# Products of k and v in unbroken rows, and wide and narrow matmuls in alternation, in a linear-attention and token-mixing block

## The chip, the cores and the metric

The kernel runs on one core of a Trainium2 chip. The core has five engines, each with its own queue in a fixed order: TensorE (PE, whose weight loads are shown as PEld), VectorE (DVE), ScalarE (ACT), GpSimd (POOL) and SyncE (SP), which issues most DMAs. They wait for each other on semaphores. The metric is the device time of one execution in microseconds (us), lower is better.

## The reference

```
def _A_ref(x, wqkv, w_phi, wo):                       # x: (1, 2048, 512), 32 heads of 16
    q, k, v = ...(x @ wqkv)...
    pq = jnp.einsum("bhsd,hdf->bhsf", q, w_phi)
    pk = jnp.einsum("bhsd,hdf->bhsf", k, w_phi)
    phi_q = jnp.concatenate([_softmax(pq, axis=-1), _softmax(-pq, axis=-1)], axis=-1)
    phi_k = jnp.concatenate([_softmax(pk, axis=-1), _softmax(-pk, axis=-1)], axis=-1)
    kv = jnp.einsum("bhsf,bhsd->bhfd", phi_k, v)
    z  = jnp.einsum("bhsf->bhf", phi_k)
    num = jnp.einsum("bhqf,bhfd->bhqd", phi_q, kv)
    den = jnp.einsum("bhqf,bhf->bhq", phi_q, z)[..., None] + 1e-6
    return (num / den)... @ wo
def _B_ref(x, w1, b1, w2, b2):                        # w1: (2048, 1792), w2: (1792, 2048)
    h = _layernorm(x, axis=-1)
    u = _gelu(jnp.einsum("bsd,sf->bdf", h, w1) + b1)
    y = jnp.einsum("bdf,fs->bds", u, w2) + b2
    return y transposed to (B, S, D)
h = x + _A_ref(_layernorm(x, axis=-1), A_wqkv, A_w_phi, A_wo)
h2 = h + _B_ref(_layernorm(h, axis=-1), B_w1, B_b1, B_w2, B_b2)
```

All values are fp32. The first half is a linear attention with a softmax feature map, the second an MLP over the token axis.

## The kernel before

The 2048 tokens are 16 tiles of 128 rows. An fp32 product is done as three products of a split operand: each operand is cut into a high part in the type fp32r and a low part (the rest), and high x high, high x low and low x high are added up in PSUM (`mm3`, L69 to L71: one wide matmul, 128x512, for each). ACT makes high parts and DVE or POOL low parts.

**Attention, about 43 to 140 us.** For each tile PE does projections of 12 wide matmuls: q (`pu`), k (`pk_ps`, already multiplied by the feature map's weights) and v (`pv`). DVE takes the maximum and the minimum of each head (L168, L169) and subtracts (L162, L166), ACT takes the exponential (L188), DVE sums it (L210), POOL normalises pk (L212) and adds it up in `zacc` (L216). ACT writes v as `vs` (L203), and the statistics of the layernorm (`sqj`, L128 and L129) and the splits of x (`xs`, L64) are on ACT too. The products of k and v, `kv(t)`, are 16 small matmuls per tile, of 32 weight columns and 64 moving columns (`kvp`, L224). They are issued in four blocks of four tiles each by `v_kv`. In this stage a scheduler orders each engine's queue: it works from the program's order, priorities and costs of its own, and may put one piece of work between others. At the end of the stage DVE adds the last tile to zacc (L499) and makes its low part (L502), PE sums it over the partitions (L510, L511), ACT writes it as zB (L512), POOL multiplies it with the q features (L461), and DVE goes on from there (L470 to L474).

**First MLP product, up to about 378 us.** It is not touched by the change, but the last stretch of it, 349 to 378 us, is ordered by the scheduler too.

**Second MLP product, from about 378 us on.** The two-by-two block product is done with seven products instead of eight (Strassen's way), so each step issues seven products with sums of blocks as operands. There are eight row blocks (`sp`) with seven steps (`p`) each. One step has six full products (`PROD`, `half` None) and one narrow one (`narrow`). A full product is a wide matmul with the high weights (`whi`, 128x512, the high and the low part of u side by side) and a narrow one with the low weights (`wlo`, 128x256), both by `wide` (L1132). `narrow` (L1136) issues three narrow matmuls. So a step is six wide and nine narrow matmuls. The weights of w2 come in 28 groups of two steps: a DMA, sums on DVE (L875 to L877), the high part by ACT (L1017, three buffers), the low part by DVE (L1027, two buffers). Three places issue the steps: at p = 0 `products` for one step, which for a single step already is wide, narrow, wide, narrow; in the middle `steps`, for one group or half of one; and at the end of a row block `products` for the last two steps (three in the last row block) together. Then ACT (L1193, L1195) and DVE (L1199 to L1204) combine the seven results and the output goes out by DMA. From the first line after `flat` on, PE, DVE and ACT keep the order in which the program is written.

Of the kernel before, what the change touches and what calls it, by code (L numbers as in the profile page):

```python
# [32 lines left out]
TURN = (6, 7, 8)  # L33
DEN_EPS = 1e-6
LAG = 5
WARM = 9
EPS = 1e-5

# [2 lines left out]
def block_kernel(ctx: ExitStack, tc: tile.TileContext, x, xT, wT, phic, wo, w1, b1, w2, b2,  # L41
# [68 lines left out]
    X, XH, EQ, PK, VS, SQ, PS, W = {}, {}, {}, {}, {}, {}, {}, {}  # L110
# [94 lines left out]
    def v_proj(t):  # L205
        v_out(t, proj(t, wvh, wvl, ps_v, "pv"))
# [11 lines left out]
    def kv(t):  # L218

        for n in range(4):  # L220
            for c in range(4):
                g = n // 2 * 4 + c
                j = 2 * g + n % 2
                nc.tensor.matmul(kvp[32 * c:32 * c + 32, n, :], VS[t][:, 32 * j:32 * j + 32],  # L224
                                 PK[t][:, g, n % 2 * 64:n % 2 * 64 + 64], start=(t == 0 and n == 0),
                                 stop=(t == NT - 1), skip_group_check=True)

    def q_sum(t):
# [5 lines left out]
    with tc.tile_pool(name="prep", bufs=1) as prep:  # L234
# [67 lines left out]
        warm = ps_k.tile([P, P], F32, name="pk_ps", tag="pk_ps")  # L302
        for _ in range(WARM):
            nc.tensor.matmul(warm, ones, ones, start=True, stop=True)
# [99 lines left out]
    def v_kv():  # L404

        nonlocal v
        v_proj(v)
        if v % 4 == 0:
            for t in range(v - 4, v):
                kv(t)  # L410
        v += 1

    v = 2
    load_h(4)
    stats_x(4)
    for t in range(3, NT - 1):
        if t + 2 < NT:
            raw = load_x(t + 2)
            load_h(t + 2)
        if t > 3:  # L420
            k_logits(t)
        if t > 3 and t not in V_NOT:
            v_kv()
        if t > 0:
            k_norm(t - 1)
        if t + 2 < NT:
            split_x(t + 2, raw)
            stats_x(t + 2)
        if t in Q_AT:
            q_mm()  # L430
            run(q_logits(0))
            q_exp(0)
            run(q_sums(1))
# [45 lines left out]
    def lead(it, mm):  # L479
# [6 lines left out]
        q_exp(0)  # L486

    v_kv()
    nc.gpsimd.tensor_add(zacc, zacc, PK[NT - 2])
    q_mm()  # L490
    k_norm(NT - 1, False)
    for j in range(KD):
        wo_hi(j)
    v_kv()
    run(q_logits(0))
    zh, zl = (kk.tile([P, NG, P], F32R, name=name, tag="pk", bufs=len(V_NOT) + 5) for name in ("zh", "zl"))
# [32 lines left out]
    for t in range(NT - 4, NT):  # L529
        kv(t)  # L530
# [157 lines left out]
    def fill_load(p):  # L688
        if FL[p] < NT:
            WI[p, FL[p]] = stream(w1v, FL[p], 2, p * 256, 256)  # L690
            FL[p] += 2

    def fill(p, pool=None):

        t = FN[p]
        FN[p] = t + 1
        if FL[p] <= t:
            fill_load(p)
        if any(part is WI[p, t - t % 2][1] for part, _, _ in LATER):
            flush()  # L700
        if t == 0:
            PU[p] = [pool.tile([P, D], F32, name="pu", tag="pu") for _ in range(2)]
        a, b = WI[p, t - t % 2]
        for c in range(2):
            mm3(PU[p][c], a[:, t % 2, c * P:(c + 1) * P], b[:, t % 2, c * P:(c + 1) * P],
                HN[t][:, 0], HN[t][:, 1], t == 0, t == NT - 1)

    def fills(it):
        if FN[1] < it - LAG:
            fill(1, ps_q)  # L710
        if FN[0] <= it - LAG:
            fill(0, ps_f)
# [12 lines left out]
    for it in range(NT + 4):  # L725
# [65 lines left out]
        for p in range(2):  # L791
            if it >= LAG - 3 + p and FL[p] <= FN[p] + 2 * (FN[p] > 0):
                fill_load(p)
# [258 lines left out]
    todo, late = [], []  # L1052
    NEAR_AT, LATE_AT = (1, 4), (2, 3, 4, 6, 8, 10)
    for n, (p, i) in enumerate(RUN):
# [12 lines left out]
        todo = todo[2:]  # L1067
# [51 lines left out]
    def products(sp, ps, order):  # L1119
        for a, b, bk, half in order:  # L1120
            if half is None:
                for low in range(2):
                    for p in ps:
                        wide(sp, p, a, b, bk, low)
            else:
                for p in ps:
                    narrow(sp, p, a, b, bk, half)

    def wide(sp, p, a, b, bk, low):
        w, u = AW[sp, p][low][:, a], UB[p, b]  # L1130
        o, u = (bank[bk][:, 0], u[:, 0]) if low else (bank[bk], u)
        nc.tensor.matmul(o, w, u, start=p == 0 and not low, stop=p == NP - 1, skip_group_check=True)  # L1132

    def narrow(sp, p, a, b, bk, half):
        for i, (x, y) in enumerate(((0, 0), (0, 1), (1, 0))):
            nc.tensor.matmul(bank[bk][:, half], AW[sp, p][x][:, a], UB[p, b][:, y], start=p == 0 and half == 0 and i == 0,  # L1136
                             stop=p == NP - 1 and i == 2, skip_group_check=True)

    def steps(sp, ps, order):
        for p in ps:  # L1140
            for a, b, bk, half in order:
                if half is None:
                    wide(sp, p, a, b, bk, 0)
        for p in ps:
            for a, b, bk, half in order:
                if half is None:
                    wide(sp, p, a, b, bk, 1)
            for a, b, bk, half in order:
                if half is not None:
                    narrow(sp, p, a, b, bk, half)  # L1150
# [6 lines left out]
    for n, (sp, p) in enumerate(STEPS):  # L1157
        t = 2 * sp
# [12 lines left out]
        order = ENDS if last else PROD  # L1171
        run_on = 3 if last else 2
        if p == 0:
            products(sp, [p], order[:-1] if n == 0 else order)
            continue
        if n == 1:
            steps(sp, [p], order[:-1])
            products(sp, [0, p], order[-1:])
            continue
        if p < NP - run_on:  # L1180
            if n % GRP == 0 or p == 1:
                steps(sp, range(p, min(p + GRP - n % GRP, NP - run_on)), order)
            continue
        if p < NP - 1:
            continue
        products(sp, range(NP - run_on, NP), order)
        e = uo.tile([P, 2, HD], F32, name="e")
        u2 = uo.tile([P, HD], F32, name="u2", bufs=1)
        u3 = uo.tile([P, HD], F32, name="u3")
        if not last:  # L1190
            ot = uo.tile([P, 2, 2, HD], F32, name="ot", bufs=1)
            low = uo.tile([P, 3, HD], F32, name="low")
# [100 lines left out]
```

## Time and profile before

| | us |
|---|---|
| median of 3 runs | 515.18 (514.93 to 515.64) |
| the profiled execution | 515.11 |
| its span in the trace | 513.3 |
| PE busy | 508.4 (99%) |
| DVE busy | 448.1 (87%) |
| ACT busy | 299.0 (58%) |
| POOL busy | 245.6 (48%) |

The difference between the execution's time and the span, 1.8 us, lies outside of what the trace shows. In the timeline a row is: start in us, the length in us, engine, line, operation, output<-inputs, weights (partitions x columns), moving size, count; in brackets the idle time of the engine just before it and what ended that. Buffer numbers are left out of names. Matmuls overlap, so that a length of 0.39 us is not the distance to the next start.

### The profile page before, as it was taken

The numbers are of one execution on the slowest core, as the hardware profiler recorded it, in microseconds if no ns is written. First come the engines' busy times: TensorE is split into PE (matmuls) and PEld (weight loads), VectorE is DVE, ScalarE is ACT, GpSimd is POOL, SyncE is SP. The second block draws the span as 40 slices with busy tenths as digits, with TensorE's granted clock in tenths as the row PEclk, the third lists the DMA queues.
The fourth block names the chain that finished last, engine by engine and source line by source line (L and its number), as shares of the span: only waits on it lengthen the run. The fifth ranks groups of instructions, "written<-read, shape, count | busy, mean of one in ns | idle before, by whom it ended". The sixth has DMA issues, their size and how long they took to land.

```text
span 513.3 us, 9312 instructions
## 1 busy us (share of the span) xinstructions
PE 508.4 (99%) x3517; PEld 437.6 (85%) x3517; DVE 448.1 (87%) x771; ACT 299.0 (58%) x498; POOL 245.6 (48%) x188
## 2 busy tenths in 40 slices
PE   8999999999999999999999999999999999999997
PEld 8888888888877787877788899998888898899897
DVE  6893999988789997877797998989999899998986
ACT  6999763435255886668976644457653444444430
POOL 2469799985999999985343200000002112211220
PEclk9999999999999999999999999999999999999999
DMA  8844311000041342434412233374135578668833
GB/s 308 278 128 119 83 43 42 1 1 3 6 161 41 103 144 83 125 123 125 138 68 86 80 107 107 100 244 129 57 123 136 151 186 163 153 138 191 173 40 78
DMA packets 36300, 58.56 MB, mean 114 GB/s; under 512 B 3744, under 2 KB 19360, under 8 KB 36256
## 3 DMA queue, kind: packets, MB, share of 16 engines
q1 hardware_dynamic: 31648, 50.85, 31.0%
q0 software_dynamic: 4032, 6.42, 9.7%
q8 instruction: 28, 0.46, 0.4%
q10 hardware_dynamic: 576, 0.69, 0.4%
q14 instruction: 16, 0.13, 0.1%
HBM read 46.81 MB, written 11.14 MB: 113 GB/s over the span
## 4 chain that ended last, share of the span: by engine, by line
PE 98%; DMA 1%; ACT 0%; SPq 0%; DVE 0%; issue 0%; ACTq 0%
PE py L1132 21%; PE pu L960 11%; PE pu L69 9%; PE pu L70 9%; PE pu L71 9%; PE py L1136 5%; PE po L71 3%; PE po L70 3%; PE po L69 3%; PE tn L557 3%; PE pk_ps L69 3%; PE pk_ps L70 3%; PE pk_ps L71 3%; PE pv L70 3%; PE pv L69 3%; PE pv L71 3%
## 5 line engine op out<-in xcount | busy, mean ns | idle before, releaser
L1208 POOL DMA_DIRECT2D out<-ot x7 | 6.2, 885 | 158.6 <-DMA wraw<-in_w 103.7
L1017 ACT ACTIVATE whi<-wraw 128x1792 fp32r<-128x1792 f32 x28 | 47.7, 1702 | 44.7 <-DVE wraw L877 26.8
L1132 PE MATMUL py<-uf,whi 128*128 128x512 f32 x225 | 61.9, 393 | 0.0
L1027 DVE TENSOR_TENSOR wlo<-wraw,whi 128x1792 fp32r<-128x1792 f32 x28 | 56.5, 2019 | 5.1 <-PE py L1136 4.9
L70 PE MATMUL pu<-hs,whi 128*128 128x512 f32 x128 | 50.2, 392 | 0.0
L69 PE MATMUL pu<-hs,whi 128*128 128x512 f32 x128 | 50.1, 399 | 0.0
L71 PE MATMUL pu<-hs,wlo 128*128 128x512 f32 x128 | 47.8, 390 | 0.0
L1132 PEld LDWEIGHTS py<-uf,whi 128*128 128x128 f32 x225 | 38.4, 189 | 4.6
L461 POOL TENSOR_TENSOR ez<-eq,zB 128x1024 f32<-128x1024 f32 x16 | 39.1, 2449 | 3.8 <-ACT zB L512 3.8
L915 ACT ACTIVATE whi<-wraw 128x896 fp32r<-128x896 f32 x24 | 22.9, 954 | 30.8 <-PE pu L960 23.6
L1132 PEld LDWEIGHTS py<-uf,wlo 128*128 128x128 f32 x225 | 35.5, 190 | 5.0
L1132 PE MATMUL py<-uf,wlo 128*128 128x256 f32 x225 | 37.5, 280 | 0.0
L960 PE MATMUL pu<-ht,whi 128*128 128x256 f32 x192 | 35.6, 283 | 0.0
L212 POOL TENSOR_TENSOR pk<-pk,sk 128x1024 f32<-128x1024 f32 x16 | 31.0, 1940 | 7.4 <-DVE sk L211 7.2
L477 POOL TENSOR_TENSOR eq<-eq,w 128x1024 f32<-128x1024 f32 x16 | 32.2, 2013 | 0.5 <-DVE w L474 0.5
L65 POOL TENSOR_TENSOR hs<-hb,hs 128x512 fp32r<-128x512 f32 x16 | 21.7, 1357 | 22.4 <-ACT hs L64 22.3
L559 ACT ACTIVATE pht<-tn 128x512 f32<-128x512 f32 x32 | 17.4, 595 | 25.5 <-PE tn L557 25.4
L216 POOL TENSOR_TENSOR zacc<-zacc,pk 128x1024 f32<-128x1024 f32 x13 | 31.2, 2402 | 0.4
L69 PEld LDWEIGHTS pu<-hs,whi 128*128 128x128 f32 x128 | 24.0, 188 | 7.1 <-issue 2.5
L960 PEld LDWEIGHTS pu<-ht,whi 128*128 128x128 f32 x192 | 29.7, 189 | 0.0
L188 ACT ACTIVATE pk<-pk,r 128x1024 f32<-128x1024 f32 x16 | 18.4, 1148 | 18.3 <-DVE pk L166 17.6
L70 PEld LDWEIGHTS pu<-hs,whi 128*128 128x128 f32 x128 | 24.1, 188 | 5.0 <-POOL hs L65 0.5
(225 smaller groups left out, 1587.7 us busy)
## 6 DMA issues: line engine op xcount, KB each, us to landing
wraw<-in_w SPq DMA_DIRECT2D x28, 512.0 KB, 4.4
wraw<-in_w SPq DMA_DIRECT2D x48, 256.0 KB, 2.8
xraw<-in_xT SPq DMA_DIRECT2D x16, 256.0 KB, 3.4
xh<-in_x SPq DMA_DIRECT2D x16, 256.0 KB, 3.0
h<-in_x SPq DMA_DIRECT2D x16, 256.0 KB, 2.7
out<-h SPq DMA_DIRECT2D x14, 256.0 KB, 3.1
out<-ot POOLq DMA_DIRECT2D x14, 256.0 KB, 4.5
wraw<-in_wT SPq DMA_DIRECT2D x12, 256.0 KB, 5.1
```

The lines of the kernel that those rows point to most:

```text
L69: nc.tensor.matmul(o, ah, bh, start=first, stop=False)
L70: nc.tensor.matmul(o, ah, bl, start=False, stop=False)
L71: nc.tensor.matmul(o, al, bh, start=False, stop=last)
L212: nc.gpsimd.tensor_mul(heads(PK[t]), heads(PK[t]), sk.unsqueeze(2).to_broadcast([P, 2 * H, DH]))
L216: nc.gpsimd.tensor_add(zacc, zacc, PK[t])
L461: nc.gpsimd.tensor_mul(EZ[t], EQ[t], zB)
L477: nc.gpsimd.tensor_mul(heads(EQ[t]), heads(EQ[t]), W[t].rearrange("p g c h -> p (g c h)").unsqueeze(2).to_broadcast([P, 2 * H, DH]))
L960: nc.tensor.matmul(ACC[p][bk][:, half], WS[p, i][x][:, a], hb[b][y], start=i == 0 and half == 0 and k == 0, stop=i == NT // 2 - 1 and k == ...
L1017: nc.scalar.activation(WH[g], RAW[g], AF.Copy)
L1027: nc.vector.tensor_sub(wl_, RAW[g], WH[g])
L1132: nc.tensor.matmul(o, w, u, start=p == 0 and not low, stop=p == NP - 1, skip_group_check=True)
L1136: nc.tensor.matmul(bank[bk][:, half], AW[sp, p][x][:, a], UB[p, b][:, y], start=p == 0 and half == 0 and i == 0, stop=p == NP - 1 and i == ...
```

## The change

It has two parts. The first is in `v_kv`: the four tiles of a block are issued under a higher priority (by 300 places of the scheduler's), and the newest of the four tiles comes first. Since tile 3 is then the first to write `kvp`, the flag that starts the accumulation goes with tile 3. The second is in `products` and `steps`. `products` goes step by step and issues for each the wide and then the narrow matmul, where it issued the wide ones of all steps and then the narrow ones. `steps` issues a wide matmul and, from the fourth on, behind each the narrow matmul of the product three places back; the last three narrow matmuls follow at the end, and then the three-matmul products of all its steps. Line numbers grow by one from L36 on, by two behind `v_kv`, and by a little more behind `steps`.

```
@@ kv @@
                 nc.tensor.matmul(kvp[32 * c:32 * c + 32, n, :], VS[t][:, 32 * j:32 * j + 32],
-                                 PK[t][:, g, n % 2 * 64:n % 2 * 64 + 64], start=(t == 0 and n == 0),
+                                 PK[t][:, g, n % 2 * 64:n % 2 * 64 + 64], start=(t == 3 and n == 0),
@@ v_kv @@
         v_proj(v)
         if v % 4 == 0:
-            for t in range(v - 4, v):
-                kv(t)
+            with tc.high_priority(offset=300):
+                for t in (v - 1, v - 4, v - 3, v - 2):
+                    kv(t)
         v += 1
@@ products @@
             if half is None:
-                for low in range(2):
-                    for p in ps:
+                for p in ps:
+                    for low in range(2):
                         wide(sp, p, a, b, bk, low)
@@ steps (BEHIND = 3) @@
     def steps(sp, ps, order):
+        todo = [(p, a, b, bk) for p in ps for a, b, bk, half in order if half is None]
+        for i in range(len(todo) + BEHIND):
+            if i < len(todo):
+                wide(sp, *todo[i], 0)
+            if i >= BEHIND:
+                wide(sp, *todo[i - BEHIND], 1)
         for p in ps:
-            for a, b, bk, half in order:
-                if half is None:
-                    wide(sp, p, a, b, bk, 0)
-        for p in ps:
-            for a, b, bk, half in order:
-                if half is None:
-                    wide(sp, p, a, b, bk, 1)
             for a, b, bk, half in order:
                 if half is not None:
                     narrow(sp, p, a, b, bk, half)
```

PE's queue around the first block of products of k and v, before (`pv` is a v projection, `pu` a q projection, `kvp` the products):

```order
L71 MATMUL pv_674<-wvh_107,xs_357 128x512
L224 MATMUL kvp_120<-pk_301,vs_409 32x64
L69 MATMUL pu_573<-wqh_87,xs_219 128x512
L224 MATMUL kvp_120<-pk_301,vs_409 32x64 x3
L70 MATMUL pu_573<-wql_88,xs_219 128x512
L71 MATMUL pu_573<-wqh_87,xs_219 128x512
...
L71 MATMUL pu_573<-wqh_87,xs_219 128x512
L224 MATMUL kvp_120<-pk_301,vs_409 32x64 x12
L224 MATMUL kvp_120<-pk_311,vs_456 32x64 x16
L224 MATMUL kvp_120<-pk_373,vs_556 32x64 x16
L224 MATMUL kvp_120<-pk_430,vs_632 32x64 x16
L69 MATMUL pu_768<-wqh_87,xs_228 128x512
```

And after:

```order
L71 MATMUL pv_674<-wvl_108,xs_357 128x512
L225 MATMUL kvp_120<-pk_430,vs_632 32x64 x16
L225 MATMUL kvp_120<-pk_301,vs_409 32x64 x16
L225 MATMUL kvp_120<-pk_311,vs_456 32x64 x16
L225 MATMUL kvp_120<-pk_373,vs_556 32x64 x16
L70 MATMUL pu_573<-wqh_87,xs_219 128x512
L71 MATMUL pu_573<-wql_88,xs_219 128x512
...
L72 MATMUL pu_573<-wqh_87,xs_219 128x512
L72 MATMUL pv_674<-wvh_107,xs_357 128x512
L70 MATMUL pu_768<-wqh_87,xs_228 128x512
```

The 64 products stand in one row, the q projection follows them in one piece, and the v projection's last matmul has moved behind that q projection. Blocks 2 to 4 stand in one row before and after.

The scheduler's new order is felt in ACT's queue at the same place, before (`vs` is v, `sqj` the statistics of a later tile, `xs` a split of x, `eq` and `pk` exponentials of q and k):

```order
L203 ACTIVATE vs_687<-pv_674,r1_66 128x512
L128 ACTIVATE sqj_970,st_971<-xh_924 128x512
L129 ACTIVATE sqj_970,st_971<-xh_924,st_971 128x512
L64 ACTIVATE xs_639<-xraw_594 128x512
L64 ACTIVATE xs_758<-xraw_649 128x512
L128 ACTIVATE sqj_1111,st_1112<-xh_1001 128x512
L129 ACTIVATE sqj_1111,st_1112<-xh_1001,st_1112 128x512
L188 ACTIVATE eq_586<-eq_586,r1_66 128x1024
L128 ACTIVATE sqj_1151,st_1152<-xh_1120 128x512
L188 ACTIVATE pk_611<-pk_611,r1_66 128x1024
L129 ACTIVATE sqj_1151,st_1152<-xh_1120,st_1152 128x512
L188 ACTIVATE pk_666<-pk_666,r1_66 128x1024
```

And after:

```order
L129 ACTIVATE sqj_1151,st_1152<-xh_1120 128x512
L204 ACTIVATE vs_687<-pv_674,r1_66 128x512
L130 ACTIVATE sqj_1151,st_1152<-xh_1120,st_1152 128x512
L65 ACTIVATE xs_639<-xraw_594 128x512
L65 ACTIVATE xs_758<-xraw_649 128x512
...
L204 ACTIVATE vs_828<-pv_815,r1_66 128x512
L189 ACTIVATE pk_611<-pk_611,r1_66 128x1024
L129 ACTIVATE sqj_1283,st_1284<-xh_1237 128x512
L65 ACTIVATE xs_835<-xraw_790 128x512
L65 ACTIVATE xs_890<-xraw_845 128x512
L204 ACTIVATE vs_883<-pv_870,r1_66 128x512
L189 ACTIVATE pk_666<-pk_666,r1_66 128x1024
```

Two tiles' statistics now stand ahead of vs_687 and of the two xs, and two more v outputs and two more xs stand ahead of the exponential of pk_666. DVE's queue in this stage is shifted in the same manner.

PE's queue in the second MLP product, a group of two steps, before (`py` is the accumulator, one number for each of the seven products, `uf` the operand of u):

```order
L1132 MATMUL py_4459<-uf_4362,whi_4216 128x512
L1132 MATMUL py_4460<-uf_4368,whi_4216 128x512
L1132 MATMUL py_4461<-uf_4362,whi_4216 128x512
L1132 MATMUL py_4463<-uf_4371,whi_4216 128x512
L1132 MATMUL py_4464<-uf_4365,whi_4216 128x512
...
L1132 MATMUL py_4465<-uf_4384,whi_4216 128x512
L1132 MATMUL py_4459<-uf_4362,wlo1_4450 128x256
L1132 MATMUL py_4460<-uf_4368,wlo1_4450 128x256
```

And after:

```order
L1134 MATMUL py_4459<-uf_4362,whi_4216 128x512
L1134 MATMUL py_4460<-uf_4368,whi_4216 128x512
L1134 MATMUL py_4461<-uf_4362,whi_4216 128x512
L1134 MATMUL py_4463<-uf_4371,whi_4216 128x512
L1134 MATMUL py_4459<-uf_4362,wlo1_4450 128x256
L1134 MATMUL py_4464<-uf_4365,whi_4216 128x512
L1134 MATMUL py_4460<-uf_4368,wlo1_4450 128x256
L1134 MATMUL py_4465<-uf_4365,whi_4216 128x512
```

The group's first narrow matmul, which needs the low weights `wlo1`, stands behind four wide ones instead of twelve. The number of matmuls is the same.

More of the change, by code (lines that the diff above doesn't have):

```diff
@@ L35 @@
 LAG = 5
+BEHIND = 3
 WARM = 9
```

## The prediction

> **What bounds the kernel now.** I read the page's busy shares and granted clock first, then its chain that ended last, then busy time by window (width, then busy us of PE, its weight loads, DVE, ACT and POOL, then the clock) over the second MLP product and the late attention stage.
>
> ```profile
> PE 508.4 (99%) x3517; PEld 437.6 (85%) x3517; DVE 448.1 (87%) x771; ACT 299.0 (58%) x498; POOL 245.6 (48%) x188
> ...
> PEclk9999999999999999999999999999999999999999
> ...
> PE 98%; DMA 1%; ACT 0%; SPq 0%; DVE 0%; issue 0%; ACTq 0%
> ```
>
> ```profile
> 378.00:494.00 116.00, 116.00 (x714) 103.90 (x713) 108.04 (x164) 50.09 (x53) 21.79 (x25) 1.00 0.65 148
> 100.00:122.60 22.60, 22.60 (x220) 18.70 (x219) 18.11 (x27) 8.64 (x11) 19.43 (x10) 1.00 0.00 1
> ```
>
> PE carries 98% of the chain at the full clock and has no idle time in either window. But a busy PE is not a PE at its closest spacing: matmuls overlap, so the only gain is a shorter distance from one start to the next. The edit leaves the matmuls' number and sizes alone; it can only close such distances, or open a wait. VectorE (DVE) is second, with 93% in the MLP window (108.04 of 116).
>
> **Part 1: products of k and v.** First block of the 32-column products in the timeline of PE (each matmul there appears as two records):
>
> ```profile
> 47.89 0.39 PE L71 MATMUL pv<-wvh,xs 128*128 128x512 f32 x1
> 48.21 0.30 PE L224 MATMUL kvp<-pk,vs 128*32 128x64 f32 x2
> 48.44 0.49 PE L69 MATMUL pu<-wqh,xs 128*128 128x512 f32 x1
> 48.86 0.31 PE L224 MATMUL kvp<-pk,vs 128*32 128x64 f32 x6
> 49.10 0.50 PE L70 MATMUL pu<-wql,xs 128*128 128x512 f32 x1
> 49.44 0.40 PE L71 MATMUL pu<-wqh,xs 128*128 128x512 f32 x1
> ...
> 51.50 0.39 PE L71 MATMUL pu<-wqh,xs 128*128 128x512 f32 x1
> 51.82 1.88 PE L224 MATMUL kvp<-pk,vs 128*32 128x64 f32 x120
> ...
> 53.97 0.39 PE L70 MATMUL pu<-wql,xs 128*128 128x512 f32 x1
> ```
>
> Six records span 0.31 us and 120 span 1.88: 1.57/114, 14 ns for each further one. Undisturbed wide projections start 0.227 us apart (134.24 to 134.92 below, three steps). From 47.89 to 49.44 there are three wide starts (0.68) and eight small records (0.11), but 1.55 us pass: the two extra switches cost 1.55 - 0.79 = 0.76 us, 0.38 each. The long piece, 51.50 to 53.97, has one switch: 2.47 - 0.45 - 1.67 = 0.35. After the change the block is one row of 64 and pays that once, so PE issues 0.76 us sooner there. Blocks 2 to 4 are unbroken already: zero. The new order of tiles asks for the newest k and v first; in block 1 the newest k is normalised by POOL long before 48, so nothing waits:
>
> ```profile
> 42.27 1.93 POOL L212 TENSOR_TENSOR pk<-pk,sk 128x1024 f32<-128x1024 f32 x1
> ```
>
> Whether the 0.76 us survive is decided at the end of the attention stage, where PE waits on a chain through all engines:
>
> ```profile
> 126.76 0.39 PE L511 MATMUL pk_ps<-zl,ones_r 128*128 128x512 f32 x1
> ...
> 134.24 0.39 PE L71 MATMUL pv<-wvh,xs 128*128 128x512 f32 x1
> ...
> 134.92 0.39 PE L71 MATMUL pv<-wvh,xs 128*128 128x512 f32 x1
> 135.20 0.47 PE L69 MATMUL pu<-wqh,xs 128*128 128x512 f32 x1
> ```
>
> ```profile
> 122.64 2.15 DVE L499 TENSOR_TENSOR zacc<-zacc,pk 128x512 f32<-128x512 f32 x2
> 124.86 1.32 DVE L502 TENSOR_TENSOR zl<-zacc,zh 128x512 fp32r<-128x512 f32 x2
> ...
> 134.37 0.68 DVE L162 TENSOR_TENSOR eq<-pu,mx 128x512 f32<-128x512 f32 x1
> ```
>
> ```profile
> 128.08 2.77 POOL L461 TENSOR_TENSOR ez<-eq,zB 128x1024 f32<-128x1024 f32 x1 [3.83 <-ACT zB L512]
> ```
>
> 134.92 to 135.20 is 0.28 instead of 0.227: PE waits there for DVE's L162, which hangs on ez (POOL), which hangs on zB and so on PE's L511 at 126.76, which needs zl. DVE ends zl at 126.18, 0.58 us before L511. So PE can come forward 0.58 us with DVE where it is, and more only if DVE's zacc comes earlier. It won't: ACT and DVE are reordered too. DVE's run through the stage starts on the moved q projection:
>
> ```profile
> 51.93 0.69 DVE L168 TENSOR_REDUCE mx<-pu 128x32 f32<-128x512 f32 x1 [2.26 <-PE pu L71]
> ```
>
> ```profile
> 51.23 1.14 ACT L64 ACTIVATE xs<-xraw 128x512 fp32r<-128x512 f32 x2
> ...
> 59.92 0.71 ACT L129 ACTIVATE sqj<-xh,st 128x512 f32<-128x512 f32 x1
> ...
> 60.63 1.14 ACT L188 ACTIVATE pk<-pk,r 128x1024 f32<-128x1024 f32 x1
> 61.67 0.67 ACT L203 ACTIVATE vs<-pv,r 128x512 f32<-128x512 f32 x1
> ```
>
> The last matmul of that q projection now follows the whole block: it starts at 51.50 plus the 120 records (1.67) plus that switch (0.35) less the two saved (0.76) less its own neighbour, which moves behind it (0.23): 52.53 instead of 51.50, so DVE starts 1.0 us later. ACT (ScalarE) now has a v output ahead of the two xs at 51.23 that needs a matmul moved behind the q projection, and ahead of the pk exponential at 60.63 now stand two more v outputs (0.67 each), the two xs of later tiles (1.14) and half of another tile's statistics (0.71): 3.2 us of work. DVE, which comes to that tile's sums in its turn, then waits about 1.0 us for it (an estimate by following both queues). Of these 2.0 us DVE can make up the 22.60 - 18.11 = 4.5 us that it idles between 100 and 122.6, as far as that idling lies in waits for others. Following its queue forward with the durations above I get zacc at 122.7 to 123.1, 0.1 to 0.5 late, hence L511 at 126.3 to 126.75. That is 0.0 to 0.46 earlier than now. I take -0.4, near the early end, because DVE's idle spells after 100 end on PE and ACT, which are then ahead. Ends: -0.76 (nothing waits), +1.4 (none of the 2.0 is made up, 2.0 - 0.58).
>
> **Part 2: alternation.** Three stretches of wide and narrow matmuls, in three orders:
>
> ```profile
> 384.84 0.40 PE L1132 MATMUL py<-uf,whi 128*128 128x512 f32 x1
> 389.73 0.40 PE L1132 MATMUL py<-un,whi 128*128 128x512 f32 x1
> ...
> 397.09 2.91 PE L1132 MATMUL py<-uf,whi 128*128 128x512 f32 x12
> 399.84 0.88 PE L1132 MATMUL py<-uf,wlo 128*128 128x256 f32 x6
> ...
> 401.99 0.40 PE L1132 MATMUL py<-uf,whi 128*128 128x512 f32 x1
> ...
> 441.17 0.40 PE L1132 MATMUL py<-un,whi 128*128 128x512 f32 x1
> ...
> 442.21 0.40 PE L1136 MATMUL py<-un,whi 128*128 128x256 f32 x2
> ...
> 443.61 0.39 PE L1132 MATMUL py<-un,whi 128*128 128x512 f32 x1
> ```
>
> 441.17 to 443.61 is a step at p=0, in strict alternation already: 2.44 us for 6 wide and 9 narrow. Twelve wide in a row and then 18 narrow, 397.09 to 401.99, take 4.90, so 2.45 for the same. The products of the last two steps, two wide and two narrow in turn, 384.84 to 389.73, take 4.89: 2.445. So alternation as it exists saves 0.02 us at each of the ten two-step rows, about 0.01 at each of seven single steps, 0.01 at each of seven closing products: 0.2 + 0.1 + 0.1 = -0.4 us.
>
> Bounds: 12 wide took 399.84 - 397.09 = 2.75, 0.229 each, while the 18 narrow took 2.15, 0.119 each. A pair in alternation takes 0.347 (three, 441.17 to 442.21, in 1.04). With wide starts at 0.227 and narrow ones at half of that a pair would be 0.340; nine pairs per two-step row, three per single step, twelve per closing product (90 + 21 + 84 = 195 pairs) then gain another 195 x 0.007 = 1.4, in all about -1.8. Narrow matmuls of another tile than the wide one just issued don't occur in this trace; if that costs each pair as much as the best case saves (+0.007), part 2 is -0.4 + 1.4 = +1.0. I take -0.4, since the p=0 rows are the same matmuls in nearly the new order.
>
> A rule that speaks against a gain: "TensorE: Matmul & The Clock Gate" in the Trainium skill, Back-to-back issue gap, gives the isolated spacing by N alone (N/2.4 + 2.5 ns, an estimate of 216 and 109 ns here); by it order is worth nothing and part 2 would be 0 (the second rival). The rows differ by order, if by half a per cent only.
>
> The new wait: the first narrow matmul of a group stands behind four wide ones instead of twelve, and needs DVE's low weights.
>
> ```profile
> 392.17 1.55 PE L1132 MATMUL py<-un,whi 128*128 128x512 f32 x6
> ...
> 394.94 0.88 PE L1132 MATMUL py<-un,wlo 128*128 128x256 f32 x6
> ```
>
> ```profile
> 390.35 0.48 DVE L1204 SCALAR_TENSOR_TENSOR ot<-py,b2s,e 128x256 f32<-128x256 f32 x1 [0.21 <-ACT low L1195]
> 390.75 2.02 DVE L1027 TENSOR_TENSOR wlo<-wraw,whi 128x1792 fp32r<-128x1792 f32 x1
> ```
>
> They end at 392.77; the narrow one starts at 394.94 now and would at 392.17 + 4 x 0.23 = 393.09. Slack shrinks from 2.17 to 0.3 us, in the tightest groups, but stays. Cost taken: 0. DVE's hold there is the outputs of the row block just finished, which come as early as their matmuls do; so it moves with PE.
>
> **Sum.** The profiled execution took 515.11 us, 0.07 under the median of 515.18. 515.11 - 0.4 - 0.4 = 514.3.
>
> **Rivals.**
> - Alternation runs at the close pair: 515.11 - 0.4 - 1.8 = 512.9. For it: wide starts tighten in a long row (0.23 to 0.227). Against: the p=0 rows don't show it within three pairs.
> - Order is worth nothing, since a start follows its predecessor by what that one's size takes: 515.11 - 0.4 = 514.7, and 515.1 if DVE's chain holds PE where it is as well. For it: the three orders lie within 0.5% (2.44 to 2.45). Against: they lie in the order of their mixing.
> - Slower, by the attention's chain: the 2.0 us that DVE starts and waits longer are not made up, PE gets zl 1.4 us later, and L162 with it: 515.11 + 1.4 - 0.4 = 516.1. It decides from zacc after 123.2 on. For it: every queue is in fixed order, and DVE is solid from 51.93 on. Against: 4.5 us of idling before 122.6.
> - Slower, by wlo: the low weights come more than 0.3 us later than now against their group, at up to nine places; 0.2 us over at each would be +1.8: 516.1 too. Against: nothing moved ahead of L1027 in DVE's queue there.
>
> **Chances.** My forecast 0.45, on its own 513.8 to 514.8; close pairs 0.27; nothing either way 0.09; attention chain 0.13; low weights 0.06. A measurement can tell about 0.2%, 1.03 us. Faster by that (under 514.15): close pairs, and nearly four tenths of the forecast, 0.44. Slower: the last two, 0.19. Within: 0.37. Range 512.9 to 516.2.
>
> **What would show it.** Right: one row of 128 records at 48.2 with a single gap on each side; zl no later than 126.2; rows of two steps in 4.88 or less; no DVE entry for wlo as a releaser of PE. Wrong: PE after 135 later than before, two-step rows at 4.90 or more, or PE idle ahead of the first narrow matmul of a group.

## The result: 0.18% slower

The changed kernel takes 516.06 us (median of 20 runs, 515.43 to 516.47), the kernel before 515.08 (20 runs, 514.60 to 515.91). The ratio is 1.0018, with a 95% interval of 1.0012 to 1.0025: it is slower, by 0.98 us. The profiled execution of the changed kernel took 516.44 us, with a span of 514.7.

From the page of the changed kernel, the chain that ended last:

```profile
PE 96%; POOL 2%; DVE 1%; issue 1%; ACT 0%; POOLq 0%
```

PE carried 98% of the chain before and carries 96% now; POOL and DVE have come into it. Where that happens is seen by following one matmul at a time. Both traces' rows of PE, before and then after: the first projection of k, the last one of k and the first q projection behind the wait (before: at 135.20, in the prediction's rows). The table below adds two later matmuls.

```profile
9.38 0.71 PE L141 MATMUL pk_ps<-wkh,xs 128*128 128x256 f32 x4
...
112.82 0.39 PE L71 MATMUL pk_ps<-wkh,xs 128*128 128x512 f32 x1
```

```profile
9.72 0.37 PE L142 MATMUL pk_ps<-wkh,xs 128*128 128x256 f32 x1
...
48.02 0.39 PE L71 MATMUL pv<-wvl,xs 128*128 128x512 f32 x1
48.34 1.99 PE L225 MATMUL kvp<-pk,vs 128*32 128x64 f32 x128
50.26 0.50 PE L70 MATMUL pu<-wqh,xs 128*128 128x512 f32 x1
...
112.38 0.39 PE L72 MATMUL pk_ps<-wkh,xs 128*128 128x512 f32 x1
...
125.63 0.39 PE L512 MATMUL pk_ps<-zh,ones_r 128*128 128x512 f32 x1
126.33 0.50 PE L513 MATMUL pk_ps<-zl,ones_r 128*128 128x512 f32 x1 [0.31 <-DVE zl L504]
126.66 0.40 PE L512 MATMUL pk_ps<-zh,ones_r 128*128 128x512 f32 x1
127.11 0.50 PE L513 MATMUL pk_ps<-zl,ones_r 128*128 128x512 f32 x1
...
135.41 0.39 PE L72 MATMUL pv<-wvh,xs 128*128 128x512 f32 x1
135.89 0.47 PE L70 MATMUL pu<-wqh,xs 128*128 128x512 f32 x1
```

| the same matmul | before | after | later by | in this stretch |
|---|---|---|---|---|
| first projection of k | 9.38 | 9.72 | 0.34 | 0.34 |
| last projection of k | 112.82 | 112.38 | -0.44 | -0.78 |
| q projection behind the wait | 135.20 | 135.89 | 0.69 | +1.13 |
| second row block's first wide matmul | 389.73 | 390.54 | 0.81 | +0.12 |
| last matmul | 509.88 | 511.20 | 1.32 | +0.51 |

The first 0.34 us isn't the change's: nothing ahead of the first projection of k is touched by any kernel here, and the same point lies at 8.80 us in the trace of `two_leads`, below:

```profile
8.80 1.38 PE L141 MATMUL pk_ps<-wkh,xs 128*128 128x256 f32 x7
```

Later times of a trace are therefore best compared from that point on; where a plain time of the changed kernel's trace is set beside one of before, 0.34 us of the difference is the start's. What is left is 0.98 us, the difference of the medians. The unbroken block gained 0.78 as predicted; 1.13 went in the waits between 125 and 136 us, and 0.6 in the second MLP product.

**The wait at the attention's end.** PE's rows above have two waits for zl (0.70 and 0.45 instead of 0.23) and one of 0.48 at 135.41, where it was 0.28. POOL's timeline after, and then the rows of before that answer to the first and the last one:

```profile
112.74 1.94 POOL L213 TENSOR_TENSOR pk<-pk,sk 128x1024 f32<-128x1024 f32 x1 [1.78 <-DVE sk L212]
114.75 2.39 POOL L217 TENSOR_TENSOR zacc<-zacc,pk 128x1024 f32<-128x1024 f32 x1
117.10 1.94 POOL L213 TENSOR_TENSOR pk<-pk,sk 128x1024 f32<-128x1024 f32 x1
119.12 2.42 POOL L491 TENSOR_TENSOR zacc<-zacc,pk 128x1024 f32<-128x1024 f32 x1
121.48 1.95 POOL L213 TENSOR_TENSOR pk<-pk,sk 128x1024 f32<-128x1024 f32 x1
```

```profile
109.33 1.94 POOL L212 TENSOR_TENSOR pk<-pk,sk 128x1024 f32<-128x1024 f32 x1 [0.57 <-DVE sk L211]
...
120.32 1.94 POOL L212 TENSOR_TENSOR pk<-pk,sk 128x1024 f32<-128x1024 f32 x1 [1.10 <-DVE sk L211]
```

Before, POOL paused 1.10 us for the sum (`sk`) of the last tile: it was ahead of DVE. Now it pauses 1.78 us instead of 0.57 ahead of tile 13's normalisation and then works through five operations without a pause, so that the last tile's is done at 123.43 instead of 122.26. The longer pause is only part of it: POOL's normalisation of tile 12 already starts at 106.53 instead of 104.34, 1.8 us late with the start's 0.34 taken off, and the pauses of before, in which that could have been made up, are gone. DVE's queue shows where the long pause comes from. Before, the rows from tile 13's sum (`sk_1348`) on:

```order
L210 TENSOR_REDUCE sk_1348<-pk_1252 128x64
L162 TENSOR_TENSOR eq_1303<-pu_1290,mx_1304 128x16x32
L166 TENSOR_TENSOR eq_1303<-mn_1305,pu_1290 128x16x32
L211 RECIPROCAL sk_1348<-sk_1348 128x64
L168 TENSOR_REDUCE mx_1326<-pk_ps_1312 128x32
L169 TENSOR_REDUCE mn_1327<-pk_ps_1312 128x32
```

And after:

```order
L169 TENSOR_REDUCE mx_1326<-pk_ps_1312 128x32
L170 TENSOR_REDUCE mn_1327<-pk_ps_1312 128x32
L211 TENSOR_REDUCE sk_1348<-pk_1252 128x64
L163 TENSOR_TENSOR pk_1325<-pk_ps_1312,mx_1326 128x16x32
L167 TENSOR_TENSOR pk_1325<-mn_1327,pk_ps_1312 128x16x32
L212 RECIPROCAL sk_1348<-sk_1348 128x64
```

The scheduler has put tile 14's four k logit operations around tile 13's sum, and all of them ahead of the reciprocal for which POOL waits. DVE's rows after, then the one of before for tz, and the group of `wol` subtractions of after and of before (in the groups: shortest, median and longest in ns, then the first and the last start):

```profile
123.47 2.20 DVE L501 TENSOR_TENSOR zacc<-zacc,pk 128x512 f32<-128x512 f32 x2 [1.11 <-POOL pk L213]
...
131.59 1.21 DVE L472 TENSOR_REDUCE tz<-ez 128x64 f32<-128x1024 f32 x1
```

```profile
130.88 1.22 DVE L470 TENSOR_REDUCE tz<-ez 128x64 f32<-128x1024 f32 x1 [2.29 <-POOL ez L461]
```

```profile
L451 DVE TENSOR_TENSOR wol<-wor,woh x4: 683/684/2885, 127.0 to 128.8; 128x512 fp32r<-128x512 f32 x4
```

```profile
L449 DVE TENSOR_TENSOR wol<-wor,woh x4: 681/682/684, 126.1 to 127.9; 128x512 fp32r<-128x512 f32 x4
```

There is a second loss. Of four equal subtractions one takes 2.89 us instead of 0.68. It starts at 128.8, behind POOL's multiplication ez:

```profile
128.42 2.70 POOL L463 TENSOR_TENSOR ez<-eq,zB 128x1024 f32<-128x1024 f32 x1 [3.30 <-ACT zB L514]
```

It ends at 131.66, 0.54 us after ez ends at 131.12, as if it had begun only then. Before, the fourth began at 127.9, ahead of ez at 128.08, and DVE then idled 2.29 us until ez was done; now it comes to `tz` 0.71 us later than before, or 0.37 with the start's 0.34 taken off. It is the same in `kv_only` and `sums_first_2`, below (2.89), and 0.69 in the traces whose fourth subtraction starts ahead of ez. The Trainium skill, "SBUF — State Buffer", section "SBUF: two separate sides", says that DVE and GpSimd share a pair of ports, that of a GpSimd operation that reads SBUF and a DVE operation with two inputs in SBUF whichever starts first holds it for its whole instruction, and that the other is blocked in full; these rows agree (0.68 us where DVE started first, 2.89 where POOL did).

**The second MLP product.** A two-step row and the closing products after it (those of the last two steps of a row block), of the changed kernel:

```profile
397.91 1.09 PE L1134 MATMUL py<-uf,whi 128*128 128x512 f32 x4
...
402.80 0.40 PE L1134 MATMUL py<-uf,whi 128*128 128x512 f32 x1
403.03 0.28 PE L1134 MATMUL py<-uf,wlo 128*128 128x256 f32 x1
...
403.86 0.40 PE L1134 MATMUL py<-uf,whi 128*128 128x512 f32 x1
...
407.76 0.40 PE L1134 MATMUL py<-un,whi 128*128 128x512 f32 x1
...
410.24 0.40 PE L1134 MATMUL py<-un,whi 128*128 128x512 f32 x1
```

The two-step row takes 4.89 us instead of 4.90, and one that stands straight behind a step at p = 0 4.89 instead of 4.91. The closing products take 4.96 (402.80 to 407.76) instead of 4.89, and the step at p = 0, whose order is unchanged, 2.48 (407.76 to 410.24) instead of 2.44. Three pairs from 402.80 on take 1.06 us, 0.353 each, where three at p = 0 took 1.04 before. That is 0.07 + 0.04 in each of six row blocks, less the 0.02 to 0.04 that its middle steps gain: 0.08 us on the average, 0.46 of the 0.51 in the last line of the table. Among PE's waits there is none for low weights.

### The profile page after: what moved, and what is told of

It reads as the page before. It is cut to its first block, busy times and chain, and to the rows that moved or that the text cites. A ratio compares the mean times of both kernels' runs of the same rounds, so it can differ in the third digit from the quotient of the medians.

```text
span 514.7 us, 9310 instructions
## 1 busy us (share of the span) xinstructions
PE 509.9 (99%) x3517; PEld 438.4 (85%) x3517; DVE 450.2 (87%) x771; ACT 299.3 (58%) x498; POOL 246.3 (48%) x188
## 4 chain that ended last, share of the span: by engine, by line
PE 96%; POOL 2%; DVE 1%; issue 1%; ACT 0%; POOLq 0%
PE py L1134 21%; PE pu L962 11%; PE pu L70 9%; PE pu L71 8%; PE pu L72 8%; PE py L1138 5%; PE po L72 3%; PE po L71 3%; PE po L70 3%; PE tn L559 3%; PE pk_ps L70 3%; PE pk_ps L71 2%; PE pk_ps L72 2%; PE pv L70 2%; PE pv L71 2%; PE pv L72 2%
## 5 line engine op out<-in xcount | busy, mean ns | idle before, releaser
L1134 PE MATMUL py<-uf,whi 128*128 128x512 f32 x225 | 76.1, 395 | 0.0
L1134 PE MATMUL py<-uf,wlo 128*128 128x256 f32 x225 | 55.5, 280 | 0.0
L1134 PEld LDWEIGHTS py<-uf,whi 128*128 128x128 f32 x225 | 41.5, 188 | 8.3
L1134 PEld LDWEIGHTS py<-uf,wlo 128*128 128x128 f32 x225 | 40.3, 189 | 1.2
L1134 PE MATMUL py<-un,whi 128*128 128x512 f32 x90 | 30.1, 396 | 0.0
L70 PEld LDWEIGHTS pu<-hs,whi 128*128 128x128 f32 x128 | 24.0, 188 | 7.1 <-issue 2.5
```

What stands on the lines that cost most here:

```text
L70: nc.tensor.matmul(o, ah, bh, start=first, stop=False)
```

## The experiments

Each is an edit of the kernel before, and the ratios are against it.

**The parts by themselves.** `kv_only` has the change to `kv` and `v_kv`, `steps_only` the new `steps`, `products_only` the new `products`, each as in the diff above.

> Only the products of k and v are changed (priority and tile order), the second MLP product stays as before. The trace of the changed kernel shows PE 0.45 us ahead at 112.8 us, or 0.8 behind what its first 10 us differ by, then 1.1 us lost between 125.6 and 135.9 where PE waits for zl and for the last subtraction. Theory: the reordered queues of DVE and POOL cost this; then this kernel alone is 0.4 us slower than before (515.5 against 515.1), with the last POOL normalisation of pk ending at 123.4 instead of 122.3. Rival: the loss there is one profile's accident; then this kernel is 0.4 to 0.8 us faster.

> Only the middle steps alternate, with the narrow matmul three products behind; the closing products and everything ahead stay as before. Theory: two-step rows take 4.88 us instead of 4.90 and single steps 2.452 instead of 2.447 to 2.460, and a step at p = 0 keeps its 2.442 us, because the loss sits in the closing products: 0.2 us faster than before. Rival: alternation in the steps leaves PE in a state in which the next step at p = 0 takes 2.480 instead of 2.442; then 0.1 us slower or the same.

> Only the closing products of the last two steps go wide, narrow, wide, narrow instead of two wide, two narrow; the middle steps and everything ahead stay as before. Theory: here sits the loss in the second MLP product, 4.957 us instead of 4.891 for each pair of closing steps, and 2.480 instead of 2.442 for the step at p = 0 behind them: 7 times 0.066 and 6 times 0.038, 0.7 us slower. Rival: the closing products are slow only behind alternating steps; then 4.89 as before and no difference.

| | median us | before | ratio | interval |
|---|---|---|---|---|
| kv_only | 515.27 | 514.95 | 1.0007 | 0.9999 to 1.0016 |
| steps_only | 514.99 | 514.95 | 1.0001 | 0.9992 to 1.0010 |
| products_only | 515.80 | 514.95 | 1.0018 | 1.0009 to 1.0027 |

The loss that the times can show sits in the closing products. The rows of `products_only` at which the closing products, the step at p = 0 behind them and the step after that begin:

```profile
419.41 0.40 PE L1132 MATMUL py<-uf,whi 128*128 128x512 f32 x1
...
424.38 0.40 PE L1132 MATMUL py<-un,whi 128*128 128x512 f32 x1
...
426.86 0.40 PE L1132 MATMUL py<-un,whi 128*128 128x512 f32 x1
```

4.97 and 2.48 us, with the middle steps as before: it isn't the alternating steps that make them slow. `steps_only` brings nothing, and its rows show why:

```profile
392.25 1.09 PE L1133 MATMUL py<-un,whi 128*128 128x512 f32 x4
...
397.20 1.09 PE L1133 MATMUL py<-uf,whi 128*128 128x512 f32 x4
```

Its two-step rows take 4.89 us instead of 4.90 where another row stands ahead of them, but straight behind a step at p = 0, as here, 4.95 instead of 4.91; a single step there takes 2.47 instead of 2.45, and closing products behind a single step 4.91 instead of 4.89. In the changed kernel, where the step at p = 0 runs in the slow rhythm of the closing products ahead of it, the same rows behind it take 4.89. So the parts don't add up: by their traces' last matmuls they lose 0.34, 0.25 and 0.81 us, 1.40 in all, where the whole change loses 0.98. The medians (0.32, 0.04 and 0.85) are too coarse to show it.

For `kv_only` the interval takes in no change at all; its trace has PE 0.79 ahead at the last projection of k (counted from the first one, as all such numbers here) and 0.34 behind from 140 us to the end.

**The order of the tiles alone.**

```
-            for t in range(v - 4, v):
+            for t in (v - 1, v - 4, v - 3, v - 2):
```

> Only the order of the four tiles within a block is changed, newest first; no priority, so the queues of DVE, ACT, POOL and SyncE are those of before and the first block stays broken in three. Both theories: no difference beyond 0.2 us. If it is slower or faster by more than that, the order of the tiles has a price of its own that I have not seen.

514.85 against 514.88 us, ratio 1.0000 (0.9991 to 1.0009). Its trace lies within 0.03 us of before at the last projection of k, behind the wait at 135 us and at the end. "Latest tile first" has no price and no gain; all of `kv_only` is the priority.

**The narrow matmul three behind in the closing products too.**

```
-        products(sp, range(NP - run_on, NP), order)
+        steps(sp, range(NP - run_on, NP), order)
```

> As the run with the middle steps alone, and the closing products too are issued with the narrow matmul three products behind, so that a wide matmul is never followed by a narrow one into its own accumulator there. Theory: what is slow in the changed kernel is a wide matmul followed by a narrow one into the same accumulator, so the closing products take 4.88 us here, and p = 0 steps stay at 2.442: 0.25 us faster than before. Rival: strict alternation as such is slow after a long stretch of it; then the closing products take 4.95 and p = 0 steps 2.480, and it is 0.5 us slower.

526.04 us, ratio 1.0222 (1.0207 to 1.0237): both expectations were wrong, by 11 us. The waits of PE's weight loads, and DVE's first operation on the results, then the same one in the kernel before:

```profile
PEld py L1133 <- DVE wlo L1028: 5.2, 7, 1.2
...
PEld py L1133 <- DVE ot L1204: 1.5, 6, 0.3
```

```profile
388.65 0.42 DVE L1196 TENSOR_TENSOR e<-py,e 128x256 f32<-128x256 f32 x1 [2.38 <-ACT e L1193]
```

```profile
386.15 0.43 DVE L1196 TENSOR_TENSOR e<-py,e 128x256 f32<-128x256 f32 x1
```

`products` finishes one accumulator after the other, and DVE and ACT combine the first while PE works on the rest. `steps` finishes all of them at the end: DVE starts 2.5 us later, its next low weights come later still, and PE waits for them and for the accumulators. This is the rival of the late low weights, on another ground than I had it. The rhythm of its closing products can be read all the same: 4.89 us, as with two and two.

**How the alternation is entered.** In `products_only` each half of the closing products starts straight behind a row of narrow matmuls, and every three pairs take 1.06 us. In `steps_only` the alternation starts behind four wide ones, and three pairs take 1.04, except in the rows straight behind a step at p = 0, where they take 1.06. `prod_lead` lets the first product go two wide, two narrow:

```
-                for low in range(2):
-                    for p in ps:
-                        wide(sp, p, a, b, bk, low)
+                for q in [ps] if bk == 0 else [[p] for p in ps]:
+                    for low in range(2):
+                        for p in q:
+                            wide(sp, p, a, b, bk, low)
```

> Closing products as in the changed kernel (wide, narrow, wide, narrow, each narrow one into the accumulator of the wide one ahead), but the first of the seven products goes two wide, two narrow as before; middle steps as before. Theory: alternation has two rhythms, 347 ns a pair and a cycle of three pairs of 1060 ns (353 each), and which one it falls into is set by how it is entered: straight out of a row of narrow ones the slow one, behind two or more wide ones the fast one. Then the closing products take 4.89 us and the p = 0 step 2.442: as before within 0.2 us. Rival: the slow rhythm comes of the same accumulator twice in a row; then 4.95 and 2.480, 0.7 us slower as with the closing products alone.

515.38 against 514.88 us, ratio 1.0008 (0.9999 to 1.0017). The rows at the beginning of its closing products, of the three-matmul products in their midst, and behind those:

```profile
419.03 0.63 PE L1133 MATMUL py<-uf,whi 128*128 128x512 f32 x2
...
421.46 0.40 PE L1137 MATMUL py<-uf,whi 128*128 128x256 f32 x2
...
423.94 0.40 PE L1133 MATMUL py<-un,whi 128*128 128x512 f32 x1
```

The first 15 matmuls, entered by two wide, take 2.43 us; the other 15, entered by one wide straight behind six narrow ones, take 2.48. Neither expectation had that halves would differ; it is the theory's case all the same, and in the kernel with two entries it is put to the test:

`steps_strict` is `steps_only` with `BEHIND = 0`.

> Middle steps in strict alternation, each narrow matmul right behind its wide one, entered straight out of a row of narrow ones; closing products as before. Theory of the entry: the slow rhythm, 12 pairs of 353 and six narrow ones of 120, 4.96 us for a two-step row instead of 4.90, and 2.48 for a single step: 10 times 0.06 and 7 times 0.03, 0.8 us slower. Rival (what counts is only how many wide and narrow ones there are): 4.88 and 2.44, faster by 0.3 us.

517.28 us, ratio 1.0045 (1.0032 to 1.0059), more than either expected, since the low weights now do come too late:

```profile
427.11 0.39 PE L1133 MATMUL py<-un,whi 128*128 128x512 f32 x1
427.76 0.38 PE L1133 MATMUL py<-un,wlo 128*128 128x256 f32 x1 [0.26 <-DVE wlo L1028]
```

```profile
PEld py L1133 <- DVE wlo L1028: 2.4, 6, 0.6
```

With one wide matmul ahead of the first narrow one PE waits at six groups, 2.4 us; with four ahead, in the changed kernel, at none. Two-step rows without a wait and entered behind narrow ones take 4.96, as expected.

**The attention's end.** `sums_first` is `kv_only` with tile 13's sum ahead of tile 14's logits on DVE, by an order that is written out from that tile on (`...` stands for lines left as they are):

```
+        if t == NT - 2:
+            nc.scalar.activation(ones_r, ones, AF.Copy)
+            ms = ExitStack()
+            ms.enter_context(tc.manual_schedule(engines={ET.PE, ET.DVE, ET.Activation, ET.Pool}))
+            o14 = proj(t, wkh, wkl, ps_k, "pk_ps")
+            v_kv()
+            k_norm(t - 1)
+            k_ops(t, o14)
+            exps(t, PK[t])
+            run(q_sums(1))
+            continue
...
-    ms = ExitStack()
-    ms.enter_context(tc.manual_schedule(engines={ET.PE, ET.DVE, ET.Activation, ET.Pool}))
-    nc.scalar.activation(ones_r, ones, AF.Copy)
```

> The change to the products of k and v alone, and DVE's sum of tile 13's exponentials (sk) put ahead of its four k logit operations for tile 14, behind which the scheduler had placed it; no change in the second MLP product. Theory: POOL idled 1.8 us for this sum at 111 us, then had 10.6 us of work in a row and ended the last normalisation 1.2 us late; with the sum 2 us earlier zacc starts at 122.6 or before instead of 123.5, the wait of PE at zl falls from 0.7 and 0.45 us to what it needs to come back to DVE's pace, and of the 0.8 us saved ahead about 0.6 stays: 0.5 to 0.6 us faster than before. Rival: DVE as a whole is late (the q logits of the moved projection), POOL only follows; then zacc stays at 123.3 or later and the time is that of the change to k and v alone, 0.3 us slower than before.

515.24 against 514.88 us, ratio 1.0005 (0.9996 to 1.0014): not the gain that I expected. It was run once more for its trace.

> The same kernel as sums_first, for its trace. The time there was 0.36 us above before, as with the change to k and v alone (0.32): the gain that was expected of an earlier sum for tile 13 did not come. Theory: POOL is no longer late (zacc starts at 122.6 or before), and another engine's work ends last ahead of zl or between zl and the subtraction at 135 us. Rival: POOL is as late as before, since its normalisations still follow one another without a pause to 123.4.

```profile
115.57 1.94 POOL L212 TENSOR_TENSOR pk<-pk,sk 128x1024 f32<-128x1024 f32 x1 [0.50 <-DVE sk L211]
...
120.99 1.94 POOL L212 TENSOR_TENSOR pk<-pk,sk 128x1024 f32<-128x1024 f32 x1 [0.99 <-DVE sk L211]
```

POOL pauses again, so the pile-up is gone, but DVE is now later itself: the logits that were put behind the sum wait for their turn, and the exponential and the next sum with them. Counted from the first projection zacc starts 0.25 us earlier than in `kv_only` and still 0.2 later than before. POOL's pile-up was only half of this delay. At 140 us the trace is 0.28 us ahead of `kv_only`'s, at the end 0.11; the times can't show that.

The other place is the slow subtraction. `kv_wol` is `kv_only` with the fourth of them behind the next q logits:

```
-    for j in range(KD):
+    for j in range(KD - 1):
         wo_lo(j)
...
     run(s_den(0))
     run(q_logits(0))
+    wo_lo(KD - 1)
     s_pq(0)
```

> The change to the products of k and v alone, and DVE's fourth subtraction for the low part of wo moved from ahead of tz to behind the next q logits (135 us). In the trace of the change alone that fourth subtraction took 2.89 us instead of 0.68, since POOL had begun ez 0.36 us before it; in the kernel before it began 0.17 us ahead of ez and took 0.68. Theory: it held DVE's tz and with it the subtraction at 135 us for 0.45 us; without it tz starts when the first ez ends, PE's gap at 135 us falls from 0.454 to 0.23 or less, and the end comes 0.2 to 0.25 us earlier than with the change alone: 0.1 us slower than before. Rival: tz is not what the subtraction waits for; then the gap at 135 us stays and nothing is gained.

515.04 against 514.95 us, ratio 1.0000 (0.9991 to 1.0009): 0.09 us above before, where `kv_only` was 0.32 above. DVE's tz, the group of subtractions and PE's rows at 135 us:

```profile
130.83 1.22 DVE L471 TENSOR_REDUCE tz<-ez 128x64 f32<-128x1024 f32 x1 [2.30 <-POOL ez L462]
```

```profile
L450 DVE TENSOR_TENSOR wol<-wor,woh x4: 684/685/918, 126.6 to 134.9; 128x512 fp32r<-128x512 f32 x4
```

```profile
135.12 0.39 PE L71 MATMUL pv<-wvh,xs 128*128 128x512 f32 x1
135.34 0.39 PE L69 MATMUL pu<-wqh,xs 128*128 128x512 f32 x1
```

DVE waits for ez alone, the moved subtraction takes 0.92, and PE's gap at 135 us is gone (0.22). The 0.23 us between the two differences are what was expected, but they lie inside the intervals; it is the traces that show it: `kv_only`'s last matmul is 0.34 us behind before, this one's level with it (-0.01), counted from the first projection.

`sums_wol` has both edits.

> As kv_wol, and DVE's sum for tile 13 ahead of the logits for tile 14 as in sums_first. Theory: two places together lose what the unbroken block saves, POOL's late normalisations (0.25 us by the trace of sums_first_2, counted from PE's first projection) and the port (0.45 us at tz); PE's gap at 135 us is 0.23, and about 0.3 of the 0.8 us stays: 0.1 to 0.3 us faster than before. Rival: a third thing keeps DVE at the pace of before; then the same as kv_wol.

514.84 against 514.95 us, ratio 0.9998 (0.9989 to 1.0007). Its trace is 0.29 us ahead of before at 140 us and 0.11 at the end, counted from the first projection; the times can't tell it from no change.

`two_leads` adds to it alternating closing products with two wide ones ahead at both entries: in `prod_lead`'s edit `bk in (0, 4)` stands for `bk == 0`.

> As sums_wol, and in the closing products wide and narrow in alternation except for the first and the fifth product (the first behind the three-matmul one), which go two wide, two narrow. Theory of the entry: both halves of the closing pair run in the fast rhythm, 2.44 each instead of 2.445, and the p = 0 step behind them takes 2.442: 0.1 us faster than sums_wol at the most, where the changed kernel with the same alternation and one wide matmul at the entry is 0.8 us slower. Rival (alternation into the same accumulator is slow by itself, and the one fast half seen was chance): 2.476 and 2.480 again in one of them, 0.5 us slower than sums_wol.

514.85 against 514.95 us, ratio 0.9995 (0.9986 to 1.0005). Its rows: both halves of the closing products, the step at p = 0, and the next one.

```profile
418.57 0.63 PE L1143 MATMUL py<-uf,whi 128*128 128x512 f32 x2
...
421.01 0.40 PE L1147 MATMUL py<-uf,whi 128*128 128x256 f32 x2
...
423.45 0.40 PE L1143 MATMUL py<-un,whi 128*128 128x512 f32 x1
...
425.89 0.63 PE L1143 MATMUL py<-un,whi 128*128 128x512 f32 x2
```

2.44, 2.44 and 2.44 us: the slow rhythm is gone, with the same alternation and the same accumulators as in the changed kernel's closing products. The first row block is the exception: there PE waits 0.2 us for low weights between the two wide matmuls and the alternation, and behind that wait three pairs take 1.06. By its ratio it is the fastest of the kernels run, by less than the measurement resolves.

## Why the prediction was wrong

I forecast 514.3 and faster; it is 516.06, on the other side. That the range holds it is luck: its upper end stood for a DVE that is 1.4 us late and for late low weights, and neither came. Both terms of the sum failed, each at one step.

- **The unbroken block, 0.76 us: right.** The trace has 0.78 by the last projection of k, and one switch on each side of 128 records.
- **"I take -0.4 for this part": wrong, it is +0.34 by the trace of `kv_only`.** The step that failed is the choice of the early end, "because DVE's idle spells after 100 end on PE and ACT, which are then ahead". The one that counts, ahead of zacc, ended on POOL (1.11 us, for pk): I had followed DVE's queue alone, and POOL, 1.8 us late by tile 12, paused 1.78 us more and found no other pause in which to make it up. So zacc started at 123.47, or 123.13 with the 0.34 of the start taken off, just past the late end of the places I had found (123.1), and the last zl matmul stands where it stood before (127.11, or 126.77, against 126.76): 0.0 instead of -0.4. The remaining 0.34 was lost behind L511, at a step that I put at nothing without a reason: I took DVE's durations from there on as fixed, and one subtraction grew from 0.68 to 2.89 us because POOL had started first. With that subtraction moved (`kv_wol`) the term is 0.0. The rival of a slower attention was there with 0.13, but priced as DVE's lateness alone (+1.4).
- **"Alternation ... -0.4": wrong, it is +0.5 to +0.6.** The failed step is the choice of the value: "since the p=0 rows are the same matmuls in nearly the new order". Those rows were entered behind two wide and two narrow matmuls. The same order entered behind a row of narrow ones runs at 0.353 a pair, which `products_only` and `prod_lead` show. Piece by piece: the middle steps gained 0.17 us in six row blocks, of the 0.3 that I had for them, the closing products took +0.07 each instead of -0.01, and the steps at p = 0, which I had counted as untouched, +0.04. My bound of +1.0 held it for a reason that isn't the one found: narrow matmuls behind a wide one of another accumulator cost nothing, since the changed kernel's two-step rows consist of them and take 4.89.
- **Low weights, cost 0: right.** No wait for them in the changed kernel. The slack of 0.3 us was real: `steps_strict`, which takes three wide matmuls of the four away, waits 2.4 us, at six groups.
- **Blocks 2 to 4 and the tile order, zero: right** (`kv_order`).
- The Trainium skill's rule on the spacing by N alone ("TensorE: Matmul & The Clock Gate", Back-to-back issue gap) would have given part 2 as 0. That is nearer than my -0.4, but the runs don't bear it out: the p = 0 step is the same row of matmuls with 2.44 and 2.48 us.

What stays open is what sets the two rhythms inside PE. The runs show that the entry decides in the closing products, and that the rhythm lasts through the few narrow matmuls in a row around the step at p = 0. They give no rule for every entry: behind the step at p = 0 the same four wide ones lead into the fast rhythm in the changed kernel and into the slow one in `steps_only`.

## What to carry to other kernels

When a scheduler orders the queues, a local gain is handed to whatever other engines it has reordered; follow every engine of the next wait's chain, those that were ahead included, and ask which of two engines now starts first where they overlap. An order that is measured in one place holds only with what stands ahead of it there. And finishing results one by one is worth more than the spacing of the matmuls that make them: 11 us here (`close_behind`) against 0.85 for the slow rhythm (`products_only`).

## What the runs showed of the hardware

- Wide (512) and narrow (256) fp32 matmuls in alternation ran in one of two rhythms, three pairs in 1.04 or in 1.06 us. Entered by one wide one straight behind six or more narrow ones it was the slow one in every row read here. Behind two wide ones it was the fast one in `prod_lead` and `two_leads`, except once, behind a wait. Behind four it was the fast one in the changed kernel, but the slow one in the rows of `steps_only` straight behind a step at p = 0. That step itself went on in the rhythm in which it was reached (2.44 or 2.48 us), its own three narrow ones notwithstanding.
- A DVE subtraction of two fp32 operands in SBUF that starts 0.36 us behind a POOL multiplication of such operands took 2.89 us, until about the end of that multiplication, instead of 0.68; one that started 0.17 us ahead of it took 0.68, and the multiplication then 2.77 instead of the 2.40 of a later one that no such subtraction overlaps (136.65 in the kernel before). DVE's subtraction from PSUM beside POOL's normalisation (121.05 in `kv_only`) took its usual 0.68.
